# Masks of two of five score groups: multiplied in by GpSimd behind the exponential instead of added by TensorE ahead of it

## The chip, the cores and the metric

The kernel runs on one core of one Trainium2 chip. The metric is the device time of one execution in microseconds; the figure for the kernel before is the median of three runs, 814.6 us (812.23 to 820.24).

## The reference

Two independent branches on 2048 tokens of width 576, whose outputs stand side by side. Branch A is sliding-window attention with 32 heads of 18 and a causal window of 256 tokens; branch B is a long convolution whose kernel comes from a state-space model (S4), by FFT.

```python
# A: q, k, v = split(x @ wqkv), 32 heads of 18
scores = einsum("bhqd,bhkd->bhqk", q, k) * 18 ** -0.5
mask = (q_idx - k_idx >= 0) & (q_idx - k_idx < 256)
scores = where(mask, scores, -1e9)
o = einsum("bhqk,bhkd->bhqd", softmax(scores), v)
a = o.transpose(...).reshape(1, 2048, 576) @ wo
# B: K = taps of the state-space model (from A, B, C, dt)
y = irfft(rfft(pad(u)) * rfft(pad(K)))[:2048] + u * Dskip
return concatenate([a, y], axis=-1)
```

The mask touches only the two edges of the window. Between them a block of 64 keys against 64 queries is wholly visible.

## The kernel before, in words

**Stages.** `build` emits four stages, each a set of streams (Python generators) whose steps are put in order by a string of letters in the table `PLAN`: one letter takes the next step of a stream, a letter with a digit takes a piece that a step has posted for another engine. So the order of every engine's instructions, and the order on SP's DMA queue, is written out by hand, and an instruction that waits holds up all that stands behind it on its engine. A second table, `SLOTS`, says which of three score buffers in PSUM ("ring", each 128 x 2 x 512 in f32, one tile in each of three pools) the next tile takes. "front" scales the inputs. "tables" projects q, k and v and builds the taps of branch B, with most of GpSimd's work (lines 555 to 574). "first" finishes the taps and begins the attention. "rest" runs the attention, the convolution and the output projection side by side.

**Attention.** It is cut into 16 items, `i` from 0 to 15: four chunks of 512 queries times four sets of eight heads. Stream `s` (`smax1`, lines 873 to 907) computes the scores of an item once to find each row's maximum: 16 ring tiles an item, each reduced by VectorE at line 907 out of PSUM. The maximum goes back into row 54 of Q by a DMA, so that the second pass gives scores minus maximum.

Stream `a` (`scores` and `score1`) is that second pass. An item's blocks of keys are packed into five groups, taken in the order 2, 4, 0, 1, 3, and each group fills two ring tiles (`pp` 0 and 1). For a tile, `score1` issues 4 matmuls for each block of keys (line 943), then 4 matmuls (line 956) that add the mask: an identity of 64 x 64 times a table `tm` of 0 and -3e38, 256 columns (128 for a few tiles of the first chunk). The four matmuls of a set work on four quarters of the array. ScalarE then takes the exponential of the whole tile into an SBUF tile `P` (line 961). Stream `v` (`pv`) multiplies the two P tiles of a group by V and adds the product up in one PSUM tile `po` an item (line 981). The row sum comes from a column of V, so P must hold zeros where the mask is. The matmuls of `pv` and of the two score passes use differently shaped pieces of the array (64x32 against 64x64).

Pool `P` has four buffers, that is, two groups. Stream `n` (`norm`) divides: `po` is copied out by ScalarE, transposed twice by VectorE (lines 1007, 1011), multiplied on GpSimd (line 1016) and split into two halves of f16 by ScalarE and GpSimd (lines 1020, 1024), and stored.

**Beside it in "rest".** The convolution: streams `c` and `d` have matmuls at lines 706 and 739; the product of the spectra is made by VectorE (line 721) and GpSimd (lines 727, 728). Stream `w` is the output projection (line 192), which closes the program: four chunks of 112 matmuls.

**GpSimd in "rest"** therefore holds 16 pairs of lines 1016 and 1024 and 24 pairs of lines 727 and 728, in one queue.

Of the kernel before, what the change touches and what calls it, by code (L numbers as in the profile page):

```python
# [13 lines left out]
I32 = mybir.dt.int32  # L14
# [28 lines left out]
def constants():  # L43
    c = {}
# [22 lines left out]
    for nm, v in mult.items():  # L67
# [9 lines left out]
    c["c_sm"], c["c_tm"] = np.concatenate([sm, sm]), np.concatenate([tm, tm])  # L77
    c["c_if"] = np.eye(128)
# [3 lines left out]
    return {k: np.ascontiguousarray(v.astype(ml_dtypes.bfloat16 if k in half else np.float32)) for k, v in c.items()}  # L82
# [4 lines left out]
        "AAAACAVVVAAVVACVACVVAVAAV1CACV1CV1AACVCVCV1PCCACV1VAACBABV1BCCPV1V1BPCPPPCP1VPP2PCP1P2BCABPPP4P4VP1C",  # L87
    "tables":
        "GMPG1GM1PG5G6PGP1PPP2GG2G5GG6P2NMPG5G6GG5MNM1G6PRG1GP1G2MMP2RPXRNM1MRUX1PPMGG1XP1P4NGPM1G2P2P4G5G5G6"
        "PP4G6X1NRXMRPP1PP2URMGX5XU1G1X1M1PUP1U2X2GPGU4P4RG5PXG2UPX1G5NMG6G6MP2U2U1PXRP1RM1X5NX4GRX2P2PXG1PMP"  # L90
        "4RX4MPGUXPPX1G2P4PM1GX1P1PUG5P1G5MP2MU1NG6P2RXPM1G6GX5NPPU2RMGP4X2G5RXPP4P1RPMU4NX1GPXG6RG1P2M1G2PX1"
        "G5P4PP1MXMG6P1X5PPM1GP2X4NX4RU4RP2PUNP4P4PP1PGMXG1X2X4PP2MG5PP1G2X1M1RPXP2PMX1G6X4P1UMGU2U1G5RM1PXG6"
        "PRP4P2RNPGPPPP4X4U4X2P4X4MG1XRX5MP1M1XUGNPX1G5PPG2X1X4XGP2MP5UPURX5G6P5X2PG5G6P4PNMU2U1RM1UPU2MXRMU1"
        "PGPPX1PPPUUPGP5M1G1PU4P5P5PU1GMRP6G5NPXU2PRG2MPG5P5G6P5PRM1P4PX1GG6MXPPXP5NPMX2X5RNRPGGG1M1P1G2PX1PM"
        "X4XMG5G5PG6P2X1X4RG6M1P1RXPPPX2P2X4NGPX4G1RMP1NPX4X5XP6RP4P2G2X1MPPM1P4U4P4MP1XMRP2GPP4G5PGM1G6PX1XP"
        "G5PG6RX4NX2UXGP1MX5X4G1X1MPPM1UPU1GRP2RP1GUXG2P4MPNU2PUU4G5PG6MP2RP1G5G6NP2X4P4PX1RM1U1PU2PMRRXP1XGM"
        "PP1P2PX5NXPX1PPM1UURX2P2MU4PX1P6X4GMPU2GPG1PX4PU1P5G5P5G2G6G5GPG6PM1PP5NRPPP4XP5PMMRX5GPPM1PP5P6G5RG"
        "1X2P5P4PXPX4X1G6GXUP5G2NMPP4MX1P6PG5RG6XM1PGPX5PNPU4PRP5P1PX2UPRPMMU4G1XU1NX4M1RGG5UPU2X1XG2PP2UMP1M"
        "PX4G6GX1PPM1PU4U1XPG5P1P2U2PRRP4G6P2GNPX5MRPUU4UMP1P2G1XX2X4PG2GU2RU1P1NM1P4RMXX1P4PG5GP1MG5PG6PP2P4"
        "G6X4X1XPP2M1PMRX2MNUPX4P1M1XPPX5X1UP2PPRP1MRMGU1XP1M1PP2U4P6P6PX1P4NP6RGPPPPU2P4G1UGG5P2PXMPPP5UG5PU"  # L100
        "4X5G6UP5U1X4P4UPP5X4G2G6NX4RP4U2PPXP5RX1MM1PX2NU4PPU2P5P4U1PPRXPX4GMP6X1MPP5U4P6M1RPG1MP5PGPP6G5PG2X"
        "P5P6GX4RXM",
    "first":
        "ssG6sG5G6M1X2RsNRMs2s2s2ssNs2ss2s2ssss2s2X1s2s2sssXRX5X1s2ss2X4ss2ss2s2s2XsX5ssss6sMs2s4s2sM1X2as2Rs"
        "2a1aXsa1X1sRs2sMRs2aXa1X1X4sXs2ss2vasX5a1vassvaa1X2s2ss2X4s2sa1s2s2s2vX4vs2ss2svX4ssssas6a1s2ssaasss"
        "s2s2s2ss2s2s2s2aa1a1sa1X4",
    "rest":
        "s2ss4kvkss2vs2s2ssvas2vv1a1aks2ka1ss2s2aasva1ca1c1vLs6aLa1aava1vnkc2css2ss2a1sc1aas2kvc3c2a1Lass2vs4"
        "va1lsss2acka1vva1sac3Lkls2vslc1s2ssas2a1dscs2s2a1sdkac2d1sc1vv1kvad1a1a1s2san3s2c2vca1Ls2vnd4svasavc"
        "1s2ad4s2s2sa1aLa1vc3s6a1lsc2Lksdsssc3s2a1vskvss2s4an1aksdsss2n6d1n3s2a1s2s2kc3assvaa1s2d1s2LsLls2ls2"  # L110
        "s2sva1svd4s2v1as2sLcs2s2s2lsa1a1s6sc1s2asvn1sasvds2kca1s2akn4Ls2a1d1vsas4sc2c1van6na1sd4c3s2va1a1s2L"
# [33 lines left out]
class Kernel:  # L145
# [671 lines left out]
    def att_setup(self):  # L817
# [5 lines left out]
        for t, n in ((self.idb, "c_id"), (self.sm, "c_sm"), (self.tm, "c_tm"), (self.idf, "c_if")):  # L823
            nc.sync.dma_start(t, a[n])
# [282 lines left out]
    def build(self):  # L1107
        nc, a = self.nc, self.a
        with ExitStack() as es:
# [58 lines left out]
            for n, b in (("m", 2), ("P", 4), ("o", 2), ("n", 1)):  # L1168
                self.pool(es, n, b, side="right")
# [61 lines left out]
```

## Time and profile before

| | |
|---|---|
| median of three runs | 814.6 us (812.23 to 820.24) |
| the profiled execution | 813.99 us, with a span of 812.2 us |
| granted TensorE clock, mean over the span | 0.956 |
| busy share of the span: PE, DVE, ACT, POOL | 87%, 74%, 66%, 45% |
| "front" | about 0 to 45 us |
| "tables" | about 45 to 365 us |
| "first" | about 365 to 400 us |
| "rest", attention and convolution | about 400 to 750 us |
| "rest", mainly the output projection | 750 to 812 us |

PE is TensorE, DVE VectorE, ACT ScalarE, POOL GpSimd, SP the engine that issues DMAs. Limits of stages are read off the trace, to some microseconds. A busy share is a union of the instructions' durations. Matmuls overlap each other, so a group's busy time on PE is more than the time by which the next group starts later; the start-to-start distance in the timeline tells that. A row of the timeline gives the start in us, the duration in us, engine, line, operation, tiles and count, and in brackets the idle time before it and what ended that.

### The profile page before, as it was taken

Reading aid. Unit: us, or ns where it says so; the run is one execution under the profiler, and the core shown is the slowest. Engines: PE = TensorE matmul, PEld = TensorE weight load, DVE = VectorE, ACT = ScalarE, POOL = GpSimd, SP = SyncE. Lnnn points to the kernel's source line nnn. Section 1 sums busy time; section 2 is a strip of 40 time slices with the busy share of each in tenths; the row PEclk is TensorE's granted clock in tenths of the full one; section 3 lists DMA queues with packets and bytes.
Section 4 is the critical chain, followed back from the end, with each engine's and each line's share of the span. In section 5 each row is a group of like instructions: output and inputs, shape, how many; then the busy total and the mean of one; then the engine's idle time right before and its main releaser. Section 6 shows DMA issues by size and latency. Waiting matters only on the chain.

```text
span 812.2 us, 29486 instructions
## 1 busy us (share of the span) xinstructions
PE 704.8 (87%) x12954; PEld 411.4 (51%) x12954; DVE 599.8 (74%) x803; ACT 534.4 (66%) x709; POOL 365.9 (45%) x285
## 2 busy tenths in 40 slices
PE   3776889988989899976788899898999998999987
PEld 2433444555445645654545454544555554466655
DVE  5997998989887698776788897678887887843010
ACT  2368676887876878553467677586778786776412
POOL 2236867885896675765004343240441353224120
PEclk9987989999999999995899999899999999999999
DMA  8897235545447638786578688569646687646674
GB/s 312 318 219 185 69 95 158 128 95 119 118 109 172 164 99 194 161 200 212 106 254 257 191 244 245 162 206 283 202 146 213 216 272 236 178 136 193 201 219 135
DMA packets 211840, 150.74 MB, mean 186 GB/s; under 512 B 103178, under 2 KB 192010, under 8 KB 211456
## 3 DMA queue, kind: packets, MB, share of 16 engines
q1 hardware_dynamic: 210096, 146.35, 63.3%
q0 software_dynamic: 1616, 2.52, 1.2%
q8 instruction: 101, 1.65, 0.9%
q14 instruction: 27, 0.22, 0.1%
HBM read 83.57 MB, written 65.11 MB: 183 GB/s over the span
## 4 chain that ended last, share of the span: by engine, by line
PE 49%; DVE 19%; ACT 15%; DMA 8%; issue 5%; SPq 3%; ACTq 0%; DVEq 0%; POOL 0%
PE po L981 7%; PE ring L192 7%; PE pp L192 7%; DVE m L907 5%; PE ring L873 4%; PE ring L739 4%; PE ring L943 4%; ACT P L961 3%; PE ring L706 3%; PE ring L603 3%; PE ring L493 2%; DMA wraw<-in_wr_dram 2%; PE ring L481 2%; DVE amx L180 2%; DMA wk<-in_c_wk_dram 2%
## 5 line engine op out<-in xcount | busy, mean ns | idle before, releaser
L907 DVE TENSOR_REDUCE m<-ring 128x2 f32<-128x640 f32 (+4 forms) x256 | 188.8, 778 | 54.1 <-PE ring L881 49.7
L961 ACT ACTIVATE P<-ring,esc 128x1024 f32<-128x1024 f32 (+2 forms) x160 | 165.8, 1061 | 72.6 <-PE ring L956 56.9
L574 POOL TENSOR_TENSOR m<-A,tr 128x1024 f32<-128x1024 f32 x72 | 142.3, 1996 | 57.6 <-DVE m L580 50.1
L981 PE MATMUL po<-P,V 64*32 64x320 f32 (+4 forms) x2816 | 98.0, 357 | 1.6 <-issue 1.5
L873 PE MATMUL ring<-K,Q 54*64 54x320 f16 (+4 forms) x1024 | 80.9, 313 | 19.3 <-DVE Q L592 6.3
L727 POOL TENSOR_TENSOR Y<-t,t 128x384 f32<-128x384 f32 x24 | 24.1, 1003 | 156.9 <-DVE t L721 144.4
L873 PEld LDWEIGHTS <-Q 54*64 54x64 f16 x1024 | 41.0, 108 | 71.5 <-issue 66.2
L943 PE MATMUL ring<-Q,K 55*64 55x320 f16 (+4 forms) x1408 | 65.4, 265 | 11.6 <-issue 4.4
L1016 POOL TENSOR_TENSOR osb<-osb,T 128x1024 f32<-128x1024 f32 x16 | 37.9, 2370 | 74.2 <-DVE T L1011 74.2
L192 PEld LDWEIGHTS <-wh 128*128 128x128 f16 x324 | 31.3, 100 | 52.2 <-issue 14.6
L192 PE MATMUL pp<-xh,wh 128*128 128x512 f16 x180 | 48.3, 400 | 10.7 <-ACT vst L393 4.6
L881 PE MATMUL ring<-sm,idb 64*64 64x128 bf16 x896 | 54.4, 222 | 0.4 <-issue 0.3
L580 DVE TENSOR_TENSOR m<-m,m 128x1024 f32<-128x1024 f32 x36 | 53.4, 1483 | 0.1
L943 PEld LDWEIGHTS <-K 55*64 55x64 f16 x1408 | 33.3, 108 | 39.3 <-issue 34.9
L603 PE MATMUL ring<-Q,m 128*32 128x64 f32 x2304 | 44.0, 233 | 10.1 <-DVE m L580 3.5
L603 PEld LDWEIGHTS ring<-Q,m 128*32 128x32 f32 x2304 | 37.8, 118 | 28.7 <-issue 9.8
L1024 POOL TENSOR_TENSOR oh<-osb,oh 128x1024 f16<-128x1024 f32 x16 | 34.2, 2135 | 39.8 <-ACT oh L1020 39.8
L981 PEld LDWEIGHTS po<-P,V 64*32 64x32 f32 x2816 | 36.6, 106 | 29.7 <-issue 22.2
L555 POOL TENSOR_TENSOR tr<-tr,mab 128x768 f32<-128x768 f32 x18 | 32.8, 1821 | 39.4 <-ACT tr L550 39.4
L192 PE MATMUL pp<-xh,wl 128*128 128x512 f16 x180 | 48.3, 402 | 0.6 <-DVE wl L360 0.6
L515 ACT ACTIVATE ring<-ring 128x1024 f32<-128x1024 f32 x36 | 36.6, 1016 | 13.7 <-PE ring L493 12.6
L956 PE MATMUL ring<-tm,idb 64*64 64x256 bf16 (+2 forms) x640 | 44.8, 258 | 0.3 <-issue 0.3
(154 smaller groups left out, 1522.3 us busy)
## 6 DMA issues: line engine op xcount, KB each, us to landing
gx<-ust SPq DMA_DIRECT2D x16, 576.0 KB
gk<-kst SPq DMA_DIRECT2D x36, 256.0 KB
xk<-gx SPq DMA_DIRECT2D x24, 384.0 KB
xk<-gk SPq DMA_DIRECT2D x24, 384.0 KB
h<-ho SPq DMA_DIRECT2D x48, 192.0 KB
hp<-h SPq DMA_DIRECT2D x24, 384.0 KB
Q<-qz SPq DMA_DIRECT2D x16, 512.0 KB
K<-kz SPq DMA_DIRECT2D x16, 512.0 KB
```

Source lines behind the costliest of these rows:

```text
L192: self.nc.tensor.matmul(ps, u, v, start=(i == 0), stop=(i == len(ops) - 1))
L574: tt(m[part], A[:, ch, a0:a0 + 8].unsqueeze(3).to_broadcast(sh), tr[:, ch, part, 0:8].unsqueeze(2).to_broadcast(sh), op=OP.mult)
L580: self.nc.vector.tensor_tensor(m[0], m[0], m[1], op=OP.add)
L603: nc.tensor.matmul(kp[32 * st:32 * st + 32, j, :], m[:, ch, 32 * term:32 * term + 32], Q[:, ch, term, :], start=(term == 0), stop=(term == ...
L873: nc.tensor.matmul(ps[z:z + 64, b, :n], d["Q"][rr, 2 * b + pp, 64 * qb:64 * qb + 64], d["K"][rr, 2 * b + pp, k0:k1], start=True, stop=Fals ...
L881: nc.tensor.matmul(out, self.idb[rr], self.sm[rr], start=False, stop=True, skip_group_check=True)
L907: self.nc.vector.tensor_reduce(out, x, axis=AX.X, op=OP.max)
L943: nc.tensor.matmul(ps[z:z + 64, b, off:off + w], d["K"][rr, 2 * b + pp, kc:kc + 64], d["Q"][rr, 2 * b + pp, q0:q0 + w], start=(k == 0), st ...
L956: nc.tensor.matmul(out, self.idb[rr], self.tm[rr, 64 * at:64 * at + n * w], start=False, stop=True, skip_group_check=True)
L961: nc.scalar.activation(P[:, :, lo:hi], ps[:, :, lo:hi], AF.Exp, scale=self.esc)
L981: nc.tensor.matmul(po[32 * p:32 * p + 32, z, q0:q0 + w], V[64 * z:64 * z + 64, kb * 76 + 19 * p:kb * 76 + 19 * p + 32], P[p % 2][64 * z:64 ...
L1016: nc.gpsimd.tensor_tensor(osb, osb, rb, op=OP.mult)
```

## The change

In groups 1 and 4 of each item (`POOLED`) the four mask matmuls go. Behind the exponential a new piece, `keep`, multiplies the masked columns of P, read as int32, by a table `mk` of 0 and 1 on GpSimd: two instructions a tile, each on 128 x 2 x 128 numbers (128 x 2 x 64 in group 1 of the first four items). Only then does the tile count as ready for `pv`. In all 256 matmuls and their 256 weight loads leave TensorE, and 128 instructions join GpSimd. An integer product with 0 gives 0 whatever the exponential of an unmasked score was, infinity too. The table `mk` is one more load of 320 KB on SP's queue. Pool `P` grows from four to eight buffers. `PLAN` and `SLOTS` are written anew throughout; their strings are left out below.

```diff
+    c["c_mk"] = np.where(c["c_tm"] == 0, 1, 0).astype(np.int32)
...
+        self.mk = ap.tile([128, 640], I32, name="mk")
...
-        for t, n in ((self.idb, "c_id"), (self.sm, "c_sm"), (self.tm, "c_tm"), (self.idf, "c_if")):
+        for t, n in ((self.idb, "c_id"), (self.sm, "c_sm"), (self.tm, "c_tm"), (self.mk, "c_mk"), (self.idf, "c_if")):
             nc.sync.dma_start(t, a[n])
...
+    POOLED = (1, 4)
...
-                    self.score1(bl, (self.MS if i >= 4 else self.MF)[n], self.sets[i % 3], pp, P)
-
-    def score1(self, bl, mask, d, pp, Ps):
+                    self.score1(bl, (self.MS if i >= 4 else self.MF)[n], self.sets[i % 3], pp, P, n in self.POOLED)
+
+    def score1(self, bl, mask, d, pp, Ps, pool):
...
-                                     d["Q"][rr, 2 * b + pp, q0:q0 + w], start=(k == 0), stop=False,
+                                     d["Q"][rr, 2 * b + pp, q0:q0 + w], start=(k == 0), stop=pool,
...
-        for b in range(2):
+        for b in range(0 if pool else 2):
...
             nc.scalar.activation(P[:, :, lo:hi], ps[:, :, lo:hi], AF.Exp, scale=self.esc)
+            if pool:
+                self.post("3", (P,), lambda: keep(P))
+            else:
+                Ps.append(P)
+
+        def keep(P):
+            for t in range(n):
+                x0 = 64 * blk + 64 * step * t
+                x = P[:, :, x0:x0 + w].bitcast(I32)
+                y = self.mk[:, 64 * at + w * t:64 * at + w * t + w].unsqueeze(1).to_broadcast([128, 2, w])
+                nc.gpsimd.tensor_tensor(x, x, y, op=OP.mult)
             Ps.append(P)
...
-            for n, b in (("m", 2), ("P", 4), ("o", 2), ("n", 1)):
+            for n, b in (("m", 2), ("P", 8), ("o", 2), ("n", 1)):
```

The new order moves instructions on every engine. Three places follow.

TensorE, item 8, group 1 (the fourth in order) in the middle of "rest", before. K is that item's keys, `po` the accumulator of an earlier item; the rows end one of the group's two score tiles and begin the other:

```order
L956 LDWEIGHTS idb
L956 MATMUL ring<-tm,idb 64x2x128
L981 MATMUL po<-P,V_4437 32x192 x8
L943 LDWEIGHTS K_4436
L943 MATMUL ring<-Q_4435,K_4436 64x128
```

The same place in the changed kernel:

```order
L948 LDWEIGHTS K_4413
L948 MATMUL ring<-Q_4412,K_4413 64x64
L948 LDWEIGHTS K_4413
L948 MATMUL ring<-Q_4412,K_4413 64x128
L948 LDWEIGHTS K_4413
```

The masks are gone, the eight `pv` matmuls between the two tiles have moved behind the second, and the two score tiles stand next to each other.

GpSimd from the end of the taps on, before (m are the last taps, Y the products of spectra, osb the division):

```order
L574 TENSOR_TENSOR m_4857<-A,tr 128x1024
L574 TENSOR_TENSOR m_4858<-A,tr 128x1024
L727 TENSOR_TENSOR Y<-t_5565,t_5566 128x384
L728 TENSOR_TENSOR Y<-t_5565,t_5566 128x384
L727 TENSOR_TENSOR Y<-t_5654,t_5655 128x384
L728 TENSOR_TENSOR Y<-t_5654,t_5655 128x384
L1016 TENSOR_TENSOR osb<-osb,T 128x1024
```

And in the middle of "rest" in the changed kernel, where the first row of masks is all of item 8's, groups 4 and 1:

```order
L1032 TENSOR_TENSOR osb<-osb,T 128x1024
L1040 TENSOR_TENSOR oh_8836<-osb,oh_8836 128x1024
L977 TENSOR_TENSOR P<-P,mk 128x2x128 x8
L730 TENSOR_TENSOR Y<-t_9330,t_9331 128x384
L731 TENSOR_TENSOR Y<-t_9330,t_9331 128x384
L1040 TENSOR_TENSOR oh_9268<-osb,oh_9268 128x1024
L977 TENSOR_TENSOR P<-P,mk 128x2x128 x4
```

The masks of a group, four instructions, stand in the queue between the products of spectra and the division.

SP's queue at the start of the attention, changed kernel:

```order
L828 DMA sm<-in_c_sm_dram 128x128
L828 DMA tm<-in_c_tm_dram 128x640
L828 DMA mk<-in_c_mk_dram 128x640
L828 DMA idf<-in_c_if_dram 128x128
L849 DMA Q_4404<-qz 128x2048
```

The load of `mk` stands ahead of the first Q, K and V; all else there is as it was.

More of the change, by code (lines that the diff above doesn't have):

```diff
@@ L88 @@
     "tables":
[L89 to L98, printed above, removed]
@@ L107 @@
+        "sMa1RXa1s2as2sX1RXX1a1ss2XX4ss2asasvX5X2s2s2aas2X4sX4ss2s2sa1vsa3a3vva1ss2s2s2sX4a1ss6a1ss2sss2ssvs2"
+        "as2a1v",
     "rest":
[L108 to L111, printed above, removed]
```

82 lines of the change are left out of this document (48 added, 34 removed).

## The prediction

> **What bounds the kernel now.** I read the busy line of the page first, then busy time by stage, then, for the stage that holds the attention, the chain of waits and the groups.
>
> ```profile
> PE 704.8 (87%) x12954; PEld 411.4 (51%) x12954; DVE 599.8 (74%) x803; ACT 534.4 (66%) x709; POOL 365.9 (45%) x285
> ...
> 45.00:365.00 320.00, 282.47 (x3605) 161.49 (x3609) 271.57 (x367) 236.36 (x375) 224.94 (x176) 0.96 0.59 141
> 365.00:400.00 35.00, 24.91 (x541) 17.17 (x535) 23.16 (x40) 14.07 (x20) 12.13 (x10) 0.59 0.55 150
> 400.00:750.00 350.00, 320.06 (x8226) 180.61 (x8227) 268.10 (x354) 249.46 (x271) 111.95 (x77) 0.99 0.71 214
> 750.00:812.00 62.00, 52.84 (x528) 36.91 (x512) 2.85 (x3) 18.50 (x23) 6.64 (x4) 0.97 0.59 185
> ```
>
> The columns are PE, PEld, DVE, ACT and POOL. From 400 to 750 us, where nearly all of the masks are, PE is busy 320 of 350 us (91%), DVE 268 (77%), ACT 249 (71%), POOL 112 (32%). So the change takes work from the fullest engine and gives it to the emptiest. But PE's share is a union of overlapping durations, and the chain says less:
>
> ```profile
> by line: PE po L981 16.7%; DVE m L907 10.2%; PE ring L739 10.2%; PE ring L873 9.8%; PE ring L943 9.2%; ACT P L961 7.1%; PE ring L706 6.5%; issue 6.1%; PE ring L192 4.1%; PE ring L802 3.3%; PE ring L956 3.0%; PE ring L881 2.5%; ACT X L714 2.
> ...
> L956 PE MATMUL ring<-tm,idb 64*64 64x256 bf16 (+2 forms) x640 | 44.8, 258 | 0.3 <-issue 0.3
> L961 ACT ACTIVATE P<-ring,esc 128x1024 f32<-128x1024 f32 (+2 forms) x160 | 165.8, 1061 | 72.6 <-PE ring L956 56.9 <-PE po L981 15.0
> L907 DVE TENSOR_REDUCE m<-ring 128x2 f32<-128x640 f32 (+4 forms) x256 | 188.8, 778 | 54.1 <-PE ring L881 49.7 <-PE ring L884 2.8
> ```
>
> The chain passes from PE to the reductions and exponentials and back: with three ring tiles, a late tile on DVE or ACT stops the next score matmul. PE leads, but not alone. The last 62 us are another matter:
>
> ```profile
> 750.78 13.98 PE ring L192 x112
> ...
> 767.57 3.35 DMA oh<-od
> ...
> 771.99 12.91 PE ring L192 x104
> ...
> 789.32 3.42 DMA oh<-od
> ...
> 792.99 14.96 PE ring L192 x108
> ```
>
> These are three chunks of the output projection with a reload between them. The change leaves them and their order as they were, so I carry them over whole, as I do the 365 us up to the attention: written anew, but with the same work, and an equal chance of either sign.
>
> **Removed: 64 sets of four mask matmuls.** The price of a set is the distance by which the next matmul on quarters of the same shape starts later:
>
> ```profile
> 614.34 0.28 PE L956 MATMUL ring<-tm,idb 64*64 64x256 bf16 x4
> 614.45 0.31 PE L873 MATMUL ring<-K,Q 54*64 54x320 f16 x4
> 614.59 0.23 PE L881 MATMUL ring<-sm,idb 64*64 64x128 bf16 x4
> 614.65 0.30 PE L873 MATMUL ring<-K,Q 54*64 54x320 f16 x4
> ...
> 614.73 1.11 ACT L961 ACTIVATE P<-ring,esc 128x1024 f32<-128x1024 f32 x1 [0.43 <-PE ring L956]
> ...
> 603.80 0.23 PE L956 MATMUL ring<-tm,idb 64*64 64x128 bf16 x4
> 603.87 0.41 PE L943 MATMUL ring<-Q,K 55*64 55x256 f16 x8
> ```
>
> That is 0.11 us for 256 columns and 0.07 for 128. Of the 64 tiles 56 have 256 columns and 8 have 128: 56 x 0.11 + 8 x 0.07 = 6.7 us. By the union (44.8 us over 640 matmuls, 0.28 a set) it would be 17.9; by the share on the chain (3.0% of 350 us, 10.5 us, of which 256 of 640 matmuls are 40%) 4.2. I take 6.7, since the start-to-start distance is what an in-order engine gains; 4.2 and 17.9 stay as ends.
>
> **Moved: the order on PE.** Where the shape of the array's pieces changes, PE waits with a weight load:
>
> ```profile
> PEld L873 <- issue: 66.2, 147, 7.1
> PEld po L981 <- issue: 22.2, 110, 0.9
> ```
>
> 22.2 / 110 = 0.20 us on the way into `pv`, and 66.2 / 147 = 0.45 before a score tile, where other things are mixed in. Counted in the two orders, behind the last taps PE has 371 runs of one shape before and 359 now. Twelve fewer at 0.20 are 2.4 us; at 0.45, 5.4; and nothing if the drain hides under a wait.
>
> **Added: buffers of P.** Who waited for `pv` (the first row) and who for exponentials (the three others):
>
> ```profile
> who waited for it (us, times):
>   ACT P L961: 15.0, 11
> ...
>   PEld ring L706: 4.6, 13
>   PE ring L943: 2.5, 8
>   PE ring L873: 2.2, 6
> ```
>
> ACT idled 15.0 us, in 11 places, for `pv` to give back a P tile. With eight buffers it need not. What PE lost to late exponentials is the other three rows and five smaller ones, some 12.6 us; 15.0 of ACT's 72.6 us of idle time are 21%, which makes 2.6. The ends are 0 and 12.6.
>
> **Added: 128 products on GpSimd.** No integer product is in the trace. The nearest rows are float products, one of them of the same size:
>
> ```profile
> L561 POOL TENSOR_TENSOR t<-tr,wi 128x256 f32<-128x256 f32 x18 | 11.3, 629 | 0.0
> L326 POOL TENSOR_TENSOR wi<-x,x 128x576 f32<-128x576 f32 x1 | 2.7, 2698 | 0.1
> ```
>
> The first gives 0.63 us. The slowest POOL row per element, the second, gives 2.70 x 256 / 576 = 1.20. I take 0.63, same size and same kind, and keep 1.20 as the far end; nothing points below 0.63. 128 x 0.63 = 81 us (a little less, 16 are half as long), and POOL goes from 112 to about 190 of 350 us: room enough, and none of it is on the path by itself. What counts is the delay to `pv`:
>
> ```profile
> 610.55 0.77 PE L981 MATMUL po<-P,V 64*32 64x320 f32 x16
> 611.35 0.33 PE L873 MATMUL ring<-K,Q 54*64 54x320 f16 x4
> ...
> 614.09 0.42 PE L943 MATMUL ring<-Q,K 55*64 55x64 f16 x12
> ```
>
> The twelve score matmuls of a tile hold PE for 0.25 us (614.09 to 614.34), and the hand-over from the end of a set to the exponential takes 0.11 (614.62 to 614.73). At item 8, group 1, the two score tiles now follow each other. Counted from the second tile, its exponential ends after 2 x 1.11 - 0.25 + 0.11; its two products need 1.26 more, 0.15 of queueing behind the first tile's, and two hand-overs of 0.11: 3.7 us in all, against 2.2 without products. In that time PE has four maximum tiles (0.20 each, 614.45 to 614.65), two score tiles with masks (0.36 each) and 24 `pv` matmuls (16 take 0.80 with the change of shape, 610.55 to 611.35; I take 1.3 for the two runs): 2.8 us. But four maximum tiles take DVE 4 x 0.82 = 3.3 us, and PE can't run far ahead of it. So such a pair comes 0.4 us late. The pairs of group 4 stand farther apart and come about even. 16 pairs x 0.4 = 6.4, half of which the ring's own stalls (30 us of idle PE in the stage) would have taken anyway: 3.2 us. The ends are 0 and 16 x (3.7 - 2.8) = 14.
>
> Behind a product that waits for its exponential stand the products Y, for which the convolution's matmuls wait, and the division. Both had long waits of their own for DVE, so I put nothing on them.
>
> **Added: the two-input collision.** In the tables stage a VectorE sum with two SBUF inputs ran beside GpSimd products:
>
> ```profile
> L580 DVE TENSOR_TENSOR m<-m,m x36: 1207/1218/2974, 76.6 to 393.0; 128x1024 f32<-128x1024 f32 x36
> L560 POOL TENSOR_TENSOR t<-tr,wr x18: 631/635/1494, 68.6 to 374.2; 128x256 f32<-128x256 f32 x18
> L721 DVE TENSOR_TENSOR t<-X x48: 934/949/989, 421.7 to 730.9; 128x768 f32<-128x768 f32 x48
> ```
>
> The first two reach over twice their median; the third, DVE's only frequent two-input work in "rest", never suffers, as POOL now mostly waits there. Products fill 81 of 350 us, so 48 x 0.23 = 11 of them meet one, for half of 0.63 us: 3.5 us on DVE. On the chain line 721 has less than the 2.5% of the last line that is printed whole, at most 8.8 of 48 x 0.95 = 46 us; that share of 3.5 is 0.7, and I take 0.5. The ends are 0 and 48 x 0.63 = 30.
>
> The Trainium skill ("SBUF — State Buffer", the section "Who interferes with whom") says that a VectorE instruction with two SBUF inputs and a GpSimd instruction that reads SBUF block each other outright, whoever came second waiting for the whole of the other. The maxima of the rows above agree with it. By that rule the change puts its products on the wrong engine wherever DVE multiplies; the rival below says what that would be.
>
> **At nothing: the load of mk and its place.** It costs SP one more issue:
>
> ```profile
> 362.97 0.43 SPq L824 DMA_DIRECT2D tm<-in_c_tm_dram  x1
> ...
> 363.92 0.43 SPq L845 DMA_DIRECT2D Q<-qz  x1
> ...
> L873 PE MATMUL ring<-K,Q 54*64 54x320 f16 (+4 forms) x1024 | 80.9, 313 | 19.3 <-DVE Q L592 6.3 <-DVE m L907 4.8 <-ACT P L961 2.2
> ```
>
> Q, K and V start 0.47 us later, and 328 KB at the stage's 150 to 214 GB/s are 1.5 to 2.2 us. The first maximum tile waited 6.3 us for DVE, which covers both; without that cover it is about 2 us.
>
> **The sum**, against the profiled execution's own 814.0 us: 814.0 - 6.7 (masks) - 2.4 (shapes) - 2.6 (buffers) + 3.2 (late pairs) + 0.5 (collision) = 806.0. That execution lies 0.6 us under the median of the runs shown.
>
> **The rivals.** *The full union.* If a set of masks holds PE for the 0.28 us that the profile counts, 814.0 - 17.9 - 2.4 - 2.6 + 3.7 = 795. For it: the exponential starts only when the set has ended. Against: the next matmul starts after 0.11. *Off the path.* If DVE and ACT set the pace, only the chain's 4.2 us come back, and buffers and shapes bring nothing: 814.0 - 4.2 + 3.7 = 813.5. For it: DVE's reductions are 10.2% of the chain. Against: PE's five attention lines together have 41%. *Collision.* Each of the 24 pairs at line 721 meets a product in full, 24 x 0.63 = 15 us on DVE, half of it on the path: 813. *GpSimd too slow, the other side.* The product costs 1.2 us. The second tile of each of 32 pairs is then 2 x 0.57 = 1.1 us later; half covered, that is 18 us: 824. It eats up the gain of 8 us from about 0.9 us a product on. For it: POOL's queue is in order, and no row shows an integer product. Against: rows of this size at 629. That the work does not move at all is excluded by the order, which shows the 128 new rows on GpSimd and 256 matmuls fewer on PE.
>
> **How the numbers follow.** The forecast has 0.55, with a range of its own of 799 to 812 us, about half of the way to the ends of its terms; off the path 0.15; collision 0.06; GpSimd too slow 0.13; full union 0.11. 1% is about what a measurement of this kernel can tell from no change (its three runs span 8 us); from the median that is 806.5 and 822.7. The forecast's centre lies just under the lower bound and its terms lean to more gain, so I put 0.36 of its 0.55 below. Faster: 0.36 + 0.11 = 0.47. Same: 0.19 + 0.15 + 0.06 = 0.40. Slower: 0.13. The range of 796 to 819 reaches nearly to the full union and halfway from the other two to the slow case, and leaves out about 2 in 10.
>
> **What would show it.** In the changed profile the products should read about 630 ns each, POOL about 190 us busy between 400 and 750, and the masks 384 matmuls. Steps are right if ACT's idle time for `pv` is gone, if `pv` waits for POOL a few microseconds in all, and if the stage from 400 us to the last three chunks is about 8 us shorter. Products of 0.9 us or more, or `pv` waiting over 10 us for POOL, make the prediction wrong upwards; a shift of more than 4 us in the first 365 us or in the last 62 makes it wrong for a reason that I left out.

## The result, and the profile after

The changed kernel takes 835.2 us (831.7 to 843.5, four runs) against 813.4 us (812.1 to 820.2): a ratio of 1.0277, with a 95% interval of 1.0222 to 1.0332. It is slower by 22 us where 8 us less had been forecast, and it lies outside the range of 796 to 819. The profiled execution took 836.2 us, with a span of 834.2. Here and below the ratios leave out executions over 1.5% above the fastest of their kernel; the medians in us include them.

First the busy line and the stages of the changed kernel. Columns of the stages: PE, PEld, DVE, ACT, POOL, granted clock, DMA share, GB/s.

```profile
PE 707.9 (85%) x12698; PEld 407.7 (49%) x12698; DVE 607.0 (73%) x803; ACT 534.2 (64%) x709; POOL 466.4 (56%) x413
```

```profile
365.00:400.00 35.00, 26.24 (x611) 18.25 (x607) 25.79 (x43) 11.19 (x15) 14.86 (x16) 0.71 0.66 163
400.00:750.00 350.00, 297.42 (x7434) 161.66 (x7434) 268.15 (x345) 231.70 (x250) 189.63 (x187) 0.95 0.66 200
750.00:840.00 90.00, 74.13 (x964) 51.86 (x962) 7.52 (x8) 33.09 (x39) 20.84 (x16) 0.96 0.56 173
```

GpSimd came to 190 of 350 us, the figure of the forecast, but in part by luck: the 115 products in that window took 86 us, where 81 us had been put for all 128, and less of GpSimd's other work lies in it (103 us, 112 before). And TensorE fell from 320 to 297 us of work in those 350, and its clock from 0.99 to 0.95: less work fitted into the same time. The last three chunks of the projection, which close the program, tell where the loss is:

```profile
774.22 13.40 PE ring L195 x108
...
794.81 12.91 PE ring L195 x104
...
814.93 15.08 PE ring L195 x108
```

They begin at 774.2 us, where they began at 750.8 before, and take about as long (60.0 us to the end of the span against 61.4). The first score tile of the attention starts at 368.5 us, where it was 372.8. So the attention and the convolution, from that tile to the last three chunks, take 405.7 us against 378.0: 27.7 us more, and all the rest is 5.7 us shorter.

The groups (count, busy us, mean ns, idle before) of the masks, the products, the exponentials and VectorE's product of the spectra:

```profile
L961 PE MATMUL ring<-tm,idb 64*64 64x256 bf16 (+2 forms) x384 | 26.9, 258 | 0.6 <-issue 0.6
L966 ACT ACTIVATE P<-ring,esc 128x1024 f32<-128x1024 f32 (+2 forms) x160 | 165.3, 1062 | 87.3 <-PE ring L961 61.6 <-PE ring L948 25.0
L977 POOL TENSOR_TENSOR P<-P,mk 128x256 int32<-128x256 int32 (+1 forms) x128 | 95.5, 774 | 127.0 <-ACT P L966 124.7 <-DMA Q<-m 2.2
L724 DVE TENSOR_TENSOR t<-X 128x768 f32<-128x768 f32 x48 | 52.9, 1141 | 10.6 <-POOL Y L731 6.6 <-ACT X L717 4.0
```

The masks are 384 matmuls, as they should be. ScalarE's 15.0 us of waiting for `pv` are gone. In the third row what counts is the last part: GpSimd stood idle for 124.7 us at the head of its queue, with a product that waited for its exponential. The fourth row was 950 ns a piece with 0.6 us of waiting; now it is 1141, and it waits 6.6 us for Y. In the kernel before it read:

```profile
L721 DVE TENSOR_TENSOR t<-X 128x768 f32<-128x768 f32 x48 | 43.6, 950 | 0.6 <-ACT X L714 0.6
```

The list of waits between 400 and 770 us (us, times, longest) shows who paid:

```profile
POOL P L977 <- ACT P L966: 105.0, 32, 8.5
...
DVE T L1023 <- POOL P L977: 12.6, 1, 12.6
...
PEld po L997 <- POOL P L977: 10.3, 10, 3.1
...
PE ring L877 <- DVE m L911: 9.4, 17, 3.5
...
PE ring L948 <- DVE m L911: 8.4, 6, 5.3
...
DVE T L1023 <- POOL osb L1032: 8.0, 2, 7.0
...
DVE t L724 <- POOL Y L731: 6.6, 2, 3.7
...
PE po L997 <- POOL P L977: 5.2, 4, 2.6
```

The same waits in the kernel before:

```profile
POOL Y L727 <- DVE t L721: 144.4, 19, 33.1
POOL osb L1016 <- DVE T L1011: 61.1, 11, 15.4
...
PE ring L873 <- DVE m L907: 4.6, 17, 0.4
...
PE ring L943 <- DVE m L907: 1.5, 6, 0.4
```

Two things are new. `pv` waits for products, 10.3 + 5.2 us. And VectorE waits for GpSimd, which it never did before in this window; with that, TensorE's waits for VectorE's maxima have grown, in the two rows shown, from 0.4 us at the longest to 5.3. VectorE's longest wait, 12.6 us, counts for little: it ends at 767.5 us, with the attention nearly over, and the kernel with group 4 alone (below) has it too and loses 0.6%.

One place shows the whole chain. The timelines of POOL, DVE and PE of the changed kernel around 660 us:

```profile
656.45 2.81 POOL L977 TENSOR_TENSOR P<-P,mk 128x256 int32<-128x256 int32 x4 [2.47 <-ACT P L966]
659.22 2.38 POOL L1032 TENSOR_TENSOR osb<-osb,T 128x1024 f32<-128x1024 f32 x1
661.56 0.99 POOL L730 TENSOR_TENSOR Y<-t,t 128x384 f32<-128x384 f32 x1
662.51 0.99 POOL L731 TENSOR_TENSOR Y<-t,t 128x384 f32<-128x384 f32 x1
663.46 2.12 POOL L1040 TENSOR_TENSOR oh<-osb,oh 128x1024 f16<-128x1024 f32 x1
```

```profile
654.55 1.80 DVE L724 TENSOR_TENSOR t<-X 128x768 f32<-128x768 f32 x2
...
659.01 0.83 DVE L911 TENSOR_REDUCE m<-ring 128x2 f32<-128x640 f32 x1 [1.92 <-PE ring L885]
663.54 3.73 DVE L724 TENSOR_TENSOR t<-X 128x768 f32<-128x768 f32 x2 [3.70 <-POOL Y L731]
667.19 2.27 DVE L911 TENSOR_REDUCE m<-ring 128x2 f32<-128x640 f32 x3
```

```profile
662.53 0.25 PE L885 MATMUL ring<-sm,idb 64*64 64x128 bf16 x4
668.05 0.64 PE L948 MATMUL ring<-Q,K 55*64 55x64 f16 x12 [5.27 <-DVE m L911]
```

VectorE had t1 and t2 ready at 656.35 (654.55 + 1.80). Y could have begun then. But GpSimd's queue had a product at its head that waited 2.47 us for its exponential, then four products, then the division, and Y began at 661.56, 5.2 us late. t1 and t2 have one buffer, so VectorE's next pair waited until Y was done (3.70 us), and then took 3.73 us in place of 1.80, beside line 1040. The maxima behind it in VectorE's queue came late, all three ring tiles were taken, and TensorE stood for 5.27 us. What follows is in the clock (the eighth column of the stages):

```profile
665.00:672.00 7.00, 3.95 (x72) 1.94 (x71) 6.06 (x8) 1.11 (x1) 2.53 (x3) 0.51 0.57 188
676.00:683.00 7.00, 7.00 (x144) 2.95 (x152) 5.27 (x8) 5.02 (x6) 5.13 (x5) 1.00 0.83 250
```

The second row is a stretch of the same length at full clock. From 2.3 us into the stall on, TensorE is granted half its clock, for 6.8 us, so that it also runs at half speed for 3.8 us after it. From 400 us to the last matmul of `pv` such stretches add up to 34.1 us in the changed kernel, in five places, and 10.2 us in two places before. By this a stall seems to take its own length and then some.

### The profile page after: what moved, and what is told of

The parts are those of the page before. It is cut to its first block, busy times and chain, and to the rows that moved or that the text cites. A ratio compares the mean times of both kernels' runs of the same rounds, so it can differ in the third digit from the quotient of the medians.

```text
span 834.2 us, 29041 instructions
## 1 busy us (share of the span) xinstructions
PE 707.9 (85%) x12698; PEld 407.7 (49%) x12698; DVE 607.0 (73%) x803; ACT 534.2 (64%) x709; POOL 466.4 (56%) x413
## 4 chain that ended last, share of the span: by engine, by line
PE 35%; DVE 15%; ACT 12%; POOL 5%; issue 4%; DMA 4%; SPq 2%; ACTq 0%; DVEq 0%; POOLq 0%
PE ring L195 7%; PE pp L195 6%; DVE m L911 6%; PE po L997 5%; ACT P L966 4%; PE ring L877 3%; PE ring L948 3%; DVE t L724 3%; POOL P L977 3%; PE ring L742 2%; PE ring L606 2%; PE ring L496 2%; PE ring L709 2%; ACT ring L518 2%; POOL osb L1032 1%
## 5 line engine op out<-in xcount | busy, mean ns | idle before, releaser
L977 POOL TENSOR_TENSOR P<-P,mk 128x256 int32<-128x256 int32 (+1 forms) x128 | 95.5, 774 | 127.0 <-ACT P L966 124.7
L997 PE MATMUL po<-P,V 64*32 64x320 f32 (+4 forms) x2816 | 103.5, 362 | 7.7 <-POOL P L977 5.2
L877 PE MATMUL ring<-K,Q 54*64 54x320 f16 (+4 forms) x1024 | 82.8, 321 | 25.5 <-DVE m L911 9.6
L877 PEld LDWEIGHTS <-Q 54*64 54x64 f16 x1024 | 42.8, 109 | 78.8 <-issue 69.9
L724 DVE TENSOR_TENSOR t<-X 128x768 f32<-128x768 f32 x48 | 52.9, 1141 | 10.6 <-POOL Y L731 6.6
L997 PEld LDWEIGHTS po<-P,V 64*32 64x32 f32 x2816 | 39.2, 107 | 42.4 <-issue 23.9
L558 POOL TENSOR_TENSOR tr<-tr,mab 128x768 f32<-128x768 f32 x18 | 34.9, 1937 | 30.5 <-ACT tr L553 30.4
L1023 DVE STREAM_TRANSPOSE T<-osb 128x1024 f32<-128x1024 f32 x16 | 19.8, 1235 | 42.9 <-ACT osb L1007 22.3
L717 ACT ACTIVATE X<-ring 128x768 f32<-128x768 f32 x48 | 36.7, 811 | 18.4 <-PE ring L709 9.1
```

The source lines that it names most:

```text
L724: tt(tm, X[:, :, :, :192].rearrange("p i s j -> p s i j"), X[:, i, :, 192:].unsqueeze(2).to_broadcast(sh), op=OP.mult)
L877: nc.tensor.matmul(ps[z:z + 64, b, :n], d["Q"][rr, 2 * b + pp, 64 * qb:64 * qb + 64], d["K"][rr, 2 * b + pp, k0:k1], start=True, stop=Fals ...
L977: nc.gpsimd.tensor_tensor(x, x, y, op=OP.mult)
L997: nc.tensor.matmul(po[32 * p:32 * p + 32, z, q0:q0 + w], V[64 * z:64 * z + 64, kb * 76 + 19 * p:kb * 76 + 19 * p + 32], P[p % 2][64 * z:64 ...
```

## The experiments

The theory after the first look: the waits in GpSimd's queue cost the time, not the products' own length. The rivals: the new order is bad; GpSimd's reads block VectorE; `pv` alone, which waits for products, takes it all. Ratios are to the kernel before, run on the same chip; 0.01 is 8.1 us. Line numbers shift by a few from kernel to kernel.

**The order alone.** The changed kernel's order, buffers and load of mk, with all masks on TensorE; the piece behind the exponential only marks the tile as ready.

```diff
-                                     d["Q"][rr, 2 * b + pp, q0:q0 + w], start=(k == 0), stop=pool,
+                                     d["Q"][rr, 2 * b + pp, q0:q0 + w], start=(k == 0), stop=False,
...
-        for b in range(0 if pool else 2):
+        for b in range(2):
...
-            for t in range(n):
-                x0 = 64 * blk + 64 * step * t
-                x = P[:, :, x0:x0 + w].bitcast(I32)
-                y = self.mk[:, 64 * at + w * t:64 * at + w * t + w].unsqueeze(1).to_broadcast([128, 2, w])
-                nc.gpsimd.tensor_tensor(x, x, y, op=OP.mult)
             Ps.append(P)
```

> The changed kernel's order, buffers and load of the table, but all masks back on TensorE and no products on GpSimd. If the new order itself is what costs, this stays at 828 us or more. If the products cost, whether by waits in GpSimd's queue or by collisions with VectorE, it lies at 805 to 818, near the kernel before.

811.5 us, ratio 0.9968 (0.9930 to 1.0005). Measured once more with more rounds:

> The changed kernel's order and eight buffers with all masks on TensorE, measured once more with more rounds (811.45 before, 0.9968 with an interval of 0.9930 to 1.0005): does it beat the kernel before? The prediction's terms for order and buffers, 2.4 + 2.6 us, would make 0.9939; the run before makes 0.9968; no gain makes 1.

814.1 us, 0.9986 (0.9953 to 1.0019). So the order isn't what costs. It and the buffers bring between 1.1 and 2.6 us, which can't be told from nothing; the forecast had 5.0. The buffers by themselves, in the order of before (`("P", 4)` made `("P", 8)`):

> The kernel before, with eight buffers of P and nothing else changed. The prediction's term: 2.6 us less, 0.9968 of the time before, ScalarE's 15 us of waiting for `pv` gone. Rival: nothing, 0.999 to 1.001, because what ScalarE waited for, TensorE did not need; then the 2.7 us of the order alone belong to the order.

812.5 us, 0.9978 (0.9937 to 1.0018): neither the 2.6 us nor nothing is excluded.

**No masks at all for groups 1 and 4.** The five lines of the product go, as above, and the mask matmuls stay away. This kernel leaves those two groups unmasked.

> As the run with the order alone, but the masks of the two groups are left out altogether, on both engines. It is the most that taking 256 matmuls from TensorE can bring in this order: 4 to 7 us under the run with the order alone if a set of four costs what the start-to-start distance says, 15 to 18 if it costs the 0.28 us of the union.

808.9 us, 0.9916 (0.9879 to 0.9954). Against the order alone that is 0.5 to 0.7% less, 4 to 6 us by ratios (2.6 by the two medians of one call), each uncertain by some 4. The 6.7 us forecast are therefore not refuted. As work they are there: the time with a matmul running, from 400 us to the end of `pv`, with what ran at half clock counted half, is 328.4 and 331.4 us in the two runs with the masks, and 321.7 without. This is also the bound of the whole idea: however the masks are made elsewhere, this order can't get below about 0.99.

**Products that nobody waits for.** 128 products of the same size on a tile of their own, with groups 1 and 4 unmasked.

```diff
+        self.dm = ap.tile([128, 2, 128], I32, name="dm")
+        nc.gpsimd.memset(self.dm, 0)
...
-                x = P[:, :, x0:x0 + w].bitcast(I32)
+                x = self.dm[:, :, 0:w]
```

> No masks on the two groups, and the 128 products run on GpSimd at the same places in its queue, but on a tile of their own, so that they wait for no exponential and no matmul waits for them. Left out is the masking itself. GpSimd has the same work and VectorE the same collisions. If collisions or GpSimd's fullness cost, this is 820 us or more; if it is the waits in the queue, it is within 5 us of the run without masks.

815.5 us, 0.9998 (0.9965 to 1.0032), that is 0.82% or 6.7 us over no products: between the two marks of the expectation. GpSimd is as busy as in the changed kernel (197 of the 350 us), and the kernel is no slower than before. Its groups:

```profile
L979 POOL TENSOR_TENSOR dm<-dm,mk 128x256 int32<-128x256 int32 (+1 forms) x128 | 96.0, 750 | 8.4
L724 DVE TENSOR_TENSOR t<-X 128x768 f32<-128x768 f32 x48 | 50.0, 1081 | 4.0 <-ACT X L717 4.0
```

GpSimd's idle time before a product is 8.4 us, not 127. VectorE's product has gone from 950 to 1081 ns. With two memsets in place of each product, which write the same tile and read nothing (in both kernels the groups stay unmasked):

```diff
-                nc.gpsimd.tensor_tensor(x, x, y, op=OP.mult)
+                for _ in range(2):
+                    nc.gpsimd.memset(x, 1)
```

> As the products that nobody reads (815.5 us, against 808.9 without any), but two memsets of the same size stand in for each product, so GpSimd is busy some 72 us without reading SBUF or waiting for anything. Groups 1 and 4 stay unmasked. Theory of the collision: the 6.7 us come from GpSimd's reads beside VectorE's, so they go, 808 to 811 us, and VectorE's product of the spectra is back from 1081 to 950 ns. Rival (mere occupancy of GpSimd's queue, which delays osb and Y): 813 to 817 us again, with VectorE's product at 950.

814.3 us by the median; by the ratio 0.9971 (0.9912 to 1.0029), which is some 811 us. The ratio lies between the two theories, and its interval takes in no masks and unread products both. VectorE's product took 1019 ns, and not the 950 that both expected. So how the 6.7 us divide into blocking and mere occupancy stays open.

**Waits without products.** Now the two memsets write 1.0 into P itself, where the product stood. They wait for the exponential and `pv` waits for them, but they read nothing and take about 0.6 us a pair. The masked columns hold 1.0 in place of 0.

> No masks on the two groups, and instead of each product two memsets of the same columns of P, which wait for the exponential and are waited for as the products are, but read no SBUF; the values there become 1. A memset of this size should take about 0.32 us, two about the length of a product. If the waits cost, this is 825 us or more, and VectorE's products of the spectra read 950 ns each again; if the collisions cost, it is within 6 us of the run without masks.

836.6 us, 1.0288 (1.0212 to 1.0364): all of the loss, with hardly any of the products.

```profile
L976 POOL MEMSET P<- 128x256 f32 (+1 forms) x256 | 71.8, 299 | 147.7 <-ACT P L966 140.3
```

This run is why the product's length is not the cause: shorter than forecast for a float product, no reads, and the same time as the changed kernel. One detail came out otherwise than expected. VectorE's product was still at 1070 ns. Sorted by what ran beside it, the 19 that met only memsets took 958 ns at most; the three of 2.78 to 2.88 us met lines 1031 and 1039 of the division, which came later and so into their way.

**`pv` waits for nothing.** The products read P, and so wait for the exponential as in the changed kernel, but write a tile of their own. `pv` waits for no product; groups 1 and 4 stay unmasked.

```diff
-                nc.gpsimd.tensor_tensor(x, x, y, op=OP.mult)
+                nc.gpsimd.tensor_tensor(self.dm[:, :, 0:w], x, y, op=OP.mult)
```

> The changed kernel, but the 128 products read P and mk and write a small tile of their own: groups 1 and 4 stay unmasked, GpSimd's queue waits for every exponential as before, and the matmuls of `pv` wait for no product. Theory (the queue: osb and Y stand behind a product that waits, VectorE waits for them, its maxima come late): nearly all of the loss stays, 828 to 838 us; the products' own wait for exponentials stays near 124 us, the two waits of VectorE for osb and Y add up to 10 us or more. Rival (`pv` itself, which waited 15.5 us for products in the changed kernel): the loss goes, 814 to 820 us, as with the products that nobody read. A time between, 820 to 828, is a split, and is read as one.

827.3 us, 1.0168 (1.0101 to 1.0235): the split that the expectation allowed for. 1.7%, 13.8 us, come with the mere waiting in the queue (over the unread products), and 1.1%, 8.9 us, are `pv`'s own wait (the rest up to the changed kernel). Theory and rival were both half right.

**Which waits of VectorE.** The hold-up should reach TensorE by VectorE's waits for osb and for Y. More buffers of T and rb take away the first, more of X, t1 and t2 the second. They need room, so P has six buffers; the control is the changed kernel with six.

```diff
-            for n, b in (("m", 2), ("P", 8), ("o", 2), ("n", 1)):
+            for n, b in (("m", 2), ("P", 6), ("o", 2), ("n", 1)):
```

> The changed kernel with 6 buffers of P, not 8; the control for the two runs that need the room. Both theories: within 0.5% of the changed kernel's 835 us (831 to 839), ScalarE waiting for `pv` by under 5 us, since the eight buffers were no part of the loss.

837.2 us, 1.0277 (1.0232 to 1.0321): the control equals the changed kernel. With `("n", 3)`:

> Six buffers of P, and three of the pair of tiles T and rb of the division, not one: VectorE's transposition of the next item need not wait until GpSimd has multiplied the item before it. Theory of the queue: VectorE's wait of 12.6 us for osb goes, and 5 to 12 us of the loss with it, 823 to 830 us. Rival (`pv`): within 3 us of the control. If the delay only moves to the next thing that the queue holds, Y, VectorE's wait for Y grows by what its wait for osb loses, and the time stays too.

837.2 us, 1.0261 (1.0181 to 1.0341): no gain, against the theory. VectorE's wait for osb is gone (8.0 us in the control; the 12.6 us of the expectation are the late wait that is put down to a product). Its wait for Y did not grow: 6.6 us, 6.3 in the control. With `("n", 1)` and `("fy", 2)`:

> Six buffers of P, and two of the tiles X, t1 and t2 of the convolution's spectra, not one: VectorE's two products of the next spectra need not wait until GpSimd has made Y of the ones before. Theory of the queue: VectorE's wait of 6.6 us for Y goes, 2 to 7 us less than the control, 828 to 834 us; TensorE's own wait for Y and the division stay. Rival (`pv`): within 2 us of the control.

834.1 us, 1.0243 (1.0204 to 1.0281): 3 us, not told apart from nothing. VectorE's wait for Y is gone, and the one for osb stays at 7.9 us. Singly the theory's waits were worth little. Both together (for room, only t1 and t2 are doubled, in a pool of their own):

```diff
-            t1 = fy.tile(sh, F32, name="t1")
-            t2 = fy.tile(sh, F32, name="t2")
+            t1 = self.p["ft"].tile(sh, F32, name="t1")
+            t2 = self.p["ft"].tile(sh, F32, name="t2")
...
-            for n, b in (("m", 2), ("P", 6), ("o", 2), ("n", 1)):
+            for n, b in (("m", 2), ("P", 6), ("o", 2), ("n", 3)):
...
-            for n, b in (("cc", 1), ("fs", 2), ("fy", 1), ("wo", 1), ("wo2", 1), ("wor", 2), ("wy", 2)):
+            for n, b in (("cc", 1), ("fs", 2), ("fy", 1), ("ft", 2), ("wo", 1), ("wo2", 1), ("wor", 2), ("wy", 2)):
```

> The changed kernel with six buffers of P, three of T and rb, and two of t1 and t2: VectorE waits neither for the division's product nor for Y. If the hold-up of GpSimd's queue reaches TensorE by way of these two waits, and each alone only moved it to the other: 8 to 12 us less than the control's 837.2, 825 to 829 us. If the single gains of 0 and 3 us were all there is: 832 to 837 us, and the hold-up takes another way.

828.2 us, 1.0175 (1.0133 to 1.0217): 1.0%, 8.3 us less than the control. The same place of the program as above, POOL and DVE and PE:

```profile
652.11 2.81 POOL L977 TENSOR_TENSOR P<-P,mk 128x256 int32<-128x256 int32 x4 [2.47 <-ACT P L966]
654.87 2.39 POOL L1032 TENSOR_TENSOR osb<-osb,T 128x1024 f32<-128x1024 f32 x1
657.20 1.73 POOL L730 TENSOR_TENSOR Y<-t,t 128x384 f32<-128x384 f32 x1
```

```profile
650.15 1.80 DVE L724 TENSOR_TENSOR t<-X 128x768 f32<-128x768 f32 x2
...
655.67 4.08 DVE L724 TENSOR_TENSOR t<-X 128x768 f32<-128x768 f32 x2
```

```profile
660.53 0.64 PE L948 MATMUL ring<-Q,K 55*64 55x64 f16 x12 [1.71 <-DVE m L911]
```

GpSimd does just the same: the wait of 2.47 us, the four products, the division, and Y again 5.3 us after t1 and t2 (657.20 against 650.15 + 1.80). But VectorE goes straight into its next pair, and TensorE's stall is 1.71 us, where it was 5.27. The group says it for the whole run:

```profile
L724 DVE TENSOR_TENSOR t<-X 128x768 f32<-128x768 f32 x48 | 52.6, 1136 | 4.1 <-ACT X L717 4.0 <-issue 0.2
```

No wait for Y is left, and the length of the piece, 1136 ns, is as bad as it was: the gain is not one of blocking. And with the products that only read P:

> The same buffers, and the products read P but write a tile of their own, so that `pv` waits for none (827.3 us without the added buffers). If VectorE's two waits are the way: about the 815.5 us of the products that wait for nothing, 813 to 819. If not: 822 to 828.

818.7 us, 1.0070 (1.0030 to 1.0110), against 1.0168 with single buffers: 0.98%, 8.0 us. So the two questions stand in a square of four kernels, in which each answer is found twice (the differences are uncertain by 0.6 to 0.9):

```
                                VectorE waits     VectorE doesn't    difference
pv waits for products           1.0277            1.0175             1.0%
pv doesn't                      1.0168            1.0070             1.0%
difference                      1.1%              1.1%
```

The traces show the way. From 400 us to the end of `pv` TensorE waited for VectorE's maxima (all lines, one execution of each kernel) 23.5 us in the changed kernel and 11.0 with both waits gone; 22.9 and 9.4 us where `pv` waits for no product; 10.9 us with unread products. With six buffers of P it was 19.4 us, and 14.9 and 15.0 with one of VectorE's two waits gone. The added buffers were not tried in the kernel before, where VectorE has neither wait; with group 4 alone (below) they bring 0.2%, which can't be told from nothing.

**Which group.** The products in one of the two groups only, the other's masks on TensorE, everything else as in the changed kernel. `real` is true for the group that is multiplied.

```diff
-        for b in range(0 if pool else 2):
+        for b in range(0 if real else 2):
...
-            for t in range(n):
+            for t in range(n if real else 0):
```

> The changed kernel's order and eight buffers, but only group 4 is multiplied on GpSimd (64 products); group 1 has its masks on TensorE again, and nothing stands in GpSimd's queue for it. If every product that waits costs alike, half of the 24 us between the order alone (811.5) and the changed kernel (835.2) comes back: 820 to 826 us. If the prediction's account of pairs holds, by which only group 1, whose two score tiles stand side by side in the order, comes late: 811 to 816 us here.

> The other half: only group 1 is multiplied on GpSimd (64 products), group 4 has its masks on TensorE. If every product that waits costs alike, 820 to 826 us. If the account of pairs holds, nearly all of the loss is here: 828 to 836 us. If the two groups' losses add up to much less than 24 us, a wait costs more where others stand beside it in the queue.

Group 4 alone: 815.8 us, 1.0033 (0.9994 to 1.0073). Group 1 alone: 830.6 us, 1.0215 (1.0132 to 1.0297). Over the order alone (0.9977, the mean of its two runs) that is 0.6% and 2.4%, and together 2.9%, where the changed kernel has 3.0%. GpSimd waited in both:

```profile
POOL P L977 <- ACT P L966: 63.8, 16, 22.5
...
DVE T L1023 <- POOL osb L1032: 8.0, 2, 7.0
```

```profile
POOL P L977 <- ACT P L966: 120.9, 17, 15.1
...
DVE t L724 <- POOL Y L731: 6.6, 2, 3.7
```

The first two rows are group 4 alone, the last two group 1 alone. A long wait at the head of the queue does little harm when nothing that is due stands behind it. VectorE's wait for osb comes with group 4, which loses little, and its wait for Y with group 1. From VectorE's second product to the start of Y, summed over the 24 pairs, pass 23.0 us in the order alone, 27.0 with group 4, 46.7 with group 1 and 49.5 in the changed kernel: it is group 1's products that stand ahead of Y. And group 1's products, read only, so that `pv` waits for none:

> Only group 1 is multiplied (830.6 us with its products in P), and its products read P but write a tile of their own. If group 1's loss of 19 us over the order alone is the hold-up of the queue: 823 to 829 us. If it is the wait of `pv`, which in group 1 stands right behind the pair: 812 to 817 us. By the split of the whole change (8 to 12) it would lie between, near 822.

830.1 us, 1.0189 (1.0131 to 1.0247): within 0.3% of the 1.0215 where `pv` waits. Group 1's loss is mostly the queue's; with intervals of 0.6 and 0.8% a part for `pv` isn't excluded.

**Does any part pay?** Group 4 alone, with VectorE's two waits taken away:

> The products of group 4 alone (its masks off TensorE, group 1's on), six buffers of P, VectorE's two waits taken away as before. If the products can pay anywhere it is here: half of the 2.6 us that the masks are worth, against half of the occupancy of 4.5 to 6.7 us and `pv`'s wait of some 6 us. By these terms 811.5 - 1.3 + 3 + 2 = 815, no better than the 815.8 without the added buffers; if VectorE's waits were what held group 4 back, 811 to 813.

815.8 us, 1.0012 (0.9986 to 1.0038). Even the harmless half, with the buffers that it needs, gives nothing. No version in which products do the masking beat the kernel before, and the order alone can't be told from it. Two things were not tried: an order in which the products of group 1 stand behind Y, and the products in the order of before, where (by a reading of that order, not by a run) one of them stands ahead of a Y on which, by way of the ring, its own exponential depends.

## Why the prediction was wrong, point by point

**The step that failed** is the sentence behind the terms: "Both had long waits of their own for DVE, so I put nothing on them." The rows were read rightly (144.4 and 61.1 us of GpSimd waiting for VectorE), and the conclusion was the wrong way round. That GpSimd waits for VectorE says that GpSimd is early, and that a late GpSimd costs GpSimd nothing. It says nothing of those who wait for GpSimd. Y and the division give back t1, t2 and rb, of which there is one each, and VectorE's next piece needs them. Nothing stood in the profile before because GpSimd had always been in time. The price of the hold-up is 1.7%, 13.8 us: 8 us by way of these two waits of VectorE (shown twice, 1.02 and 0.98%), and 5.9 us (0.72%, from the unread products at 0.9998 to 1.0070) that remain when both are gone, uncertain by 4. Where those go by is open. In the two traces TensorE's waits for exponentials differ, 11.4 us with unread products and 16.8 us here, and ScalarE waits 5.6 us for tiles of P here and not there; this kernel has six of them and not eight, so a part may be the buffers' and not the queue's.

**Masks, -6.7.** The work is there (6.7 and 9.7 us of TensorE's time at full clock). Of it 4 to 6 us by ratios reached the end. Right within the uncertainty.

**Shapes and buffers, -2.4 and -2.6.** Together -1.1 and -2.6 in two measurements, the buffers alone -1.8, none told apart from nothing. ScalarE's wait did go; it had been worth little.

**Late pairs, +3.2.** `pv`'s wait costs 8.7 us (1.09 and 1.05%), inside the bounds of 0 to 14, and the term was mis-sized. Halving it because the ring stalls anyway was too kind, and the 6.4 us that were halved were too few as well: TensorE waited 15.5 us for products, more than the 10 that the text had set as the sign of its being wrong. That group 1 would be late and group 4 about even was right of the groups, but group 1 pays by way of the queue.

**Collision, +0.5.** Products that nobody waits for cost 6.7 us (2.6 to 10.8). The term held VectorE's direct delay against its share on the chain, and had no part for the division and Y, which come later when GpSimd is busier; how much of the 6.7 us each of the two has is open. The rival of 15 us on VectorE, half of it on the path, was the better figure, but by luck: VectorE's products grew by 6.4 us (43.6 to 50.0). VectorE's product, with two SBUF inputs, was stretched to 2.9 us beside the division, which reads SBUF on GpSimd, and not at all by memsets: all 25 products that met nothing but memsets, in two kernels, took 958 ns or less. The Trainium skill ("SBUF — State Buffer", "Who interferes with whom") exempts a GpSimd instruction that only writes SBUF from the blocking. The traces agree.

**The product itself** took 731 ns by the median where 630 was estimated, well under the 0.9 us from which the gain was to be eaten up. So the rival "GpSimd too slow" had the right sign and came nearest in time (824), but not by the cause: memsets of 0.6 us a pair in its place gave the same 1.0288. It named GpSimd's in-order queue among its evidence, and priced only `pv`'s wait by it.

**The parts left as they were.** The start of the attention moved by 4.3 us to the better, just over the 4 that were set, and the end by 1.4: the loss is not there. Nor is the 4.3 a gain to rely on: with the same start, the runs above have that tile anywhere from 367.6 to 373.6 us.

The terms as measured make the sum: no masks for the two groups 0.9916; products on GpSimd +0.82%; their waiting in the queue +0.72%, and by way of VectorE's two waits +1.0%; `pv` +1.07%; that is 1.0277. They must add up, since each is a difference of two runs in a row. Without the step that failed, and with the other sizes right, the forecast would have been 0.9916 + 0.0082 + 0.0107 = 1.0105, some 822 us: still slower. Two errors of size had the same sign as the error of reasoning.

## What to carry to other kernels

Before work is put on an idle engine, list not only what the new instruction waits for but what stands behind it in that engine's queue, and for each of these who gets a buffer or a result from it; a wait of that engine for another is no slack for those who wait for it. Work that depends on a late engine goes behind what is due earlier (not tried here), or its neighbours in the queue get a second buffer of what they give back (worth 1.0% here, not enough to make the change pay). And when two waits are fed by one hold-up, try taking them away together as well: singly they showed 0.2 and 0.3% here (uncertain by 0.6 to 0.9), together 1.0%, which is not proof that together is more than the sum.

## What the runs showed of the hardware

Stretches at half clock go with stalls of TensorE; they lasted 3.4, 6.8 or 10.2 us. In the changed kernel there were five between 400 us and the end of `pv`. Four began inside a stall: 2.3 us into the one of 5.27 us, 2.1 us into the one of 3.48 us at 451 us, in the second of three near 610 us, and 1.4 us into one of 2.58 us at 715 us. The fifth began right behind one of 2.04 us at 509 us. Each outlasted its stall by some us. In the 3.4 us before each of the five, a matmul had been running for 20 to 53% of the time. A stall of 1.95 us at 548 us brought none. TensorE's idle time and the time in which it worked at half clock, both from 400 us to the end of `pv` in one execution of each kernel, rise together, though loosely:

```
                             idle, us    working at half clock, us    ratio
order alone                  30.0        9.3                          0.9968
order alone, again           31.9        13.7                         0.9986
no masks                     33.8        16.4                         0.9916
unread products              36.7        18.1                         0.9998
group 4 alone                36.9        16.7                         1.0033
both waits gone, read only   42.3        18.8                         1.0070
both waits gone              43.6        24.7                         1.0175
group 1, read only           44.1        38.7                         1.0189
group 1 alone                46.3        29.9                         1.0215
read only                    48.8        22.5                         1.0168
memsets in P                 51.9        38.5                         1.0288
changed kernel               54.0        24.3                         1.0277
```

Half of the second column is lost. Between the first row and the last the stage grows by 28.4 us: 24.0 of idle time and 7.5 of half clock, less 3.2 of work. So between these two executions a microsecond of stall cost about 1.3; other rows would give other figures. That the gaps bring on the half clock is argued from their order in time and was not tried by itself. The Trainium skill ("TensorE: Matmul & The Clock Gate", "What's actually happening") has the clock halved after at least one idle window of about 3.4 us. The traces here don't bear that length out: a stall of 2.04 us at 509 us was enough.

The worst case of the blocking, at 448 us of the changed kernel (timelines of POOL and DVE):

```profile
448.07 2.38 POOL L1032 TENSOR_TENSOR osb<-osb,T 128x1024 f32<-128x1024 f32 x1
450.57 2.68 POOL L1040 TENSOR_TENSOR oh<-osb,oh 128x1024 f16<-128x1024 f32 x1
```

```profile
448.50 5.57 DVE L724 TENSOR_TENSOR t<-X 128x768 f32<-128x768 f32 x2
```

Two products of 1.8 us in all took 5.57, one behind each of GpSimd's two pieces. In the kernel before no product of VectorE took over 989 ns; with the products in GpSimd's queue, waiting or unread (2.87 us at the longest there too), the division comes later and meets them.
